# GpSimd writes the ones beside batch 2's and 3's value rows, batch 3's loads stand earlier, and pair 2's maxima stand behind the masks of pairs 0 and 1

## The chip, the cores and the metric

One Trainium2 chip, one core. The metric is the device time of one launch in microseconds (us); lower is better. The times of the kernel before are three runs; the profile is one more execution.

## What is computed

The inputs are q, k and v of shape (4, 8, 768, 64) (batch, heads, sequence, head size) and the weights of a gated layer. The reference, cut to what matters:

```python
k_sum = k.reshape(B, H, nb, 32, D).max(axis=3)      # 24 block maxima
v_sum = v.reshape(B, H, nb, 32, D).mean(axis=3)     # 24 block means
scores_l = scale * q @ k.T, kept only where |i - j| < 16
scores_s = scale * q @ k_sum.T + log(32)
a = softmax(concat([scores_l, scores_s]))
x = a @ concat([v, v_sum])                          # heads side by side: (3072, 512)
h = x @ w_in;  g = h * sigmoid(beta * h);  out = g @ w_out
```

d_model is 512 and d_ff is 2048. All matmuls run in bf16, the output is float32.

## The kernel before

The four batches run one after the other, and the work of batch b+1's attention is woven into batch b's two big matmuls. Heads are handled in pairs: pair g of a batch holds heads 2g and 2g+1, so there are four pairs. For each batch TensorE (PE) runs `h_group` (x times w_in, 16 groups, L509) and then `o_part` (times w_out, 24 parts, L530). On this main list a side list of small steps is laid: `at_time(t, f, ...)` puts step f at a planned time t, the list is sorted by t, and each step is emitted ahead of the first main step whose planned time is not below t. The planned times are only numbers that set an order: each engine then runs its own instructions in that order and waits for semaphores. `up` is the planned end of the h groups of the batch.

For batches 2 and 3 (while batch 1 or 2 is in the big matmuls) the steps of one pair are:

- `load_next` (on GpSimd, "POOL", which issues the DMAs that cast float32 to bf16): `load_v` brings value rows into `ve` (L118, the first and last rows apart in L126 and L124), `load_row` brings k and q rows in natural layout (L111, two DMAs each, 96 KB each). In front of pair 0 the columns `D:VW` of rows 96 to 127 of `ve` are set to one, so that the matmul that averages v also sums. There are two `ve` buffers, so batch 3's rows replace batch 1's, and four buffers each for k rows and q rows, so batch 3's pair g replaces batch 2's pair g.
- `copy_v` (on SyncE's queue, "SP"): two DMAs copy `ve` into `vo`, shifted by half a chunk (L328).
- `cross` (SP): two transposing DMAs bring k and q rows into `kw` and `qt` (L303, L305).
- `max_k` and `rows_k` (VectorE, "DVE"): the block maxima of the keys (L311, L313), then two copies that build the second set of key rows (L319, L320).
- `mean_v` (PE, L340) and `rows_v` (DVE, L347 and L353): block means of v, written into rows 96 to 127 of `ve` and `vo`.
- `scores` for two pairs (PE, L438, then exp on ScalarE, "ACT", L440), `mask` (DVE, L447), `av` (PE, L464), `norm` (DVE, L473 and L474), and `x_transpose` (SP, a transposing DMA into `xT`, L483). `xT` of all four pairs is what the next batch's h groups read; pair g is the g-th of the four products that are summed.

`scores` takes three accumulators and each `av` one, all from the same three "big" buffers, so the next `scores` needs `norm` of the `av` before it. SP also issues the stores of the output rows (L551), in its own order. The first two h groups of a batch are begun with pairs 0 to 2 only and finished with pair 3.

The block that plans batches 2 and 3 (`nxt` is the batch that is prepared; L685 to L703):

```python
elif nxt is not None:
    for g in pairs:
        at_time(0.1 + 0.2 * g, copy_v, nxt, g)
        at_time(0.2 + 0.2 * g, cross, nxt, g)
        m = 3.9 + 3.9 * g if g < 3 else up + 2.0
        at_time(m, max_k, nxt, g)
        at_time(m, rows_k, nxt, g)
    at_time(14.0, mean_v, nxt, pairs)
    for g in pairs:
        at_time(14.1 + 1.0 * g, rows_v, nxt, g)
    for g0, t, a in ((0, up + 0.8, up + 5.9), (2, up + 9.0, up + 14.5)):
        at_time(t, scores, nxt, g0)
        for g in (g0, g0 + 1):
            at_time(t, mask, nxt, g)
            at_time(a, av, (nxt, g), 0, nch)
        for g in (g0, g0 + 1):
            at_time(a, norm, (nxt, g), nch)
            at_time(a, x_transpose, (nxt, g), 0, nch, "big", dve)
```

Of the kernel before, what the change touches and what calls it, by code (L numbers as in the profile page):

```python
# [12 lines left out]
def kernel(  # L13
# [10 lines left out]
    nc = tc.nc  # L24
    ctx.enter_context(tc.manual_schedule(engines={getattr(mybir.EngineType, e) for e in ("SP", "Pool", "PE", "DVE", "Activation")}))
    P = 128
# [5 lines left out]
    B, H, S, D = q.shape  # L32
# [15 lines left out]
    VW = D + 1  # L48
# [7 lines left out]
    SUM = 96  # L56
# [18 lines left out]
    HC = H * nch  # L75
    PC = 2 * nch
    ve_bufs = [const.tile([P, HC + 1, VW], bf16, name=f"ve{i}") for i in range(2)]
# [30 lines left out]
    def load_row(nm, b, g):  # L108
        t = qk_pool.tile([P, nch, 2, D], bf16, name=nm + "_nat", tag=nm + "_row")
        for h in range(2):  # L110
            nc.gpsimd.dma_start(out=t[:, :, h], in_=(k_row if nm == "k" else q_row)[b, g, :, h])  # L111
        nat[(nm, b, g)] = t

    def load_v(b, g, n=1):
        lo, hi = PC * g + 1, min(PC * (g + n) + 1, HC)
        rows = v[b].rearrange("h s d -> (h s) d")
        src = rows[lo * P - W:hi * P - W].rearrange("(c p) d -> p c d", p=P)
        nc.gpsimd.dma_start(out=ve_bufs[b % 2][:, lo:hi, 0:D], in_=src)  # L118

    def load_v_edge(b, last):  # L120
        ve = ve_bufs[b % 2]
        rows = v[b].rearrange("h s d -> (h s) d")
        if last:
            nc.gpsimd.dma_start(out=ve[0:W, HC, 0:D], in_=rows[H * S - W:H * S])  # L124
        else:
            nc.gpsimd.dma_start(out=ve[W:P, 0, 0:D], in_=rows[0:P - W])  # L126
# [370 lines left out]
    def h_group(u, i, ks=range(k1)):  # L497

        b, t0, w = units[u]
        nn = 2 // w  # L500
        if 0 in ks:
            if (i * nn) % (k2 // w) == 0:
                h_bufs[(u, i * nn * w // k2)] = moe_pool.tile([P, k2 // w, w * MG], bf16, name="h_sb", tag="h_sb", bufs=4)
            h_open[(u, i)] = ps.tile([P, 2, 512], f32, name="h_ps", tag="big", bufs=3)
        big = h_open[(u, i)]
        for j in range(2):
            ni, tok = (i, t0 + j * MG) if w == 2 else (2 * i + j, t0)
            for ki in ks:
                nc.tensor.matmul(big[:, j, 0:MG], w_in_sb[:, ki, ni * P:(ni + 1) * P], xT[b][:, ki, tok:tok + MG],  # L509
                                 start=(ki == 0), stop=(ki == k1 - 1))  # L510
        if k1 - 1 not in ks:
            return
        for j in range(nn):
            ni = i * nn + j
            hb = h_bufs[(u, ni * w // k2)][:, ni % (k2 // w)]
            nc.scalar.activation(out=hb.rearrange("p (k m) -> p k m", m=MG), in_=big[:, j:j + w, 0:MG],  # L516
                                 func=ACTF.Silu, scale=beta_sb[:, ni:ni + 1])
# [119 lines left out]
    for b in range(B):  # L637
        us = [u for u, z in enumerate(units) if z[0] == b]
        up = sum(NG[u] for u in us) * GT
        total = up + nch * 4 * OT  # L640
        nxt = b + 1 if b + 1 < B else None
        pairs = tuple(range(npair))
        side = []

        def at_time(t, f, *a):
            side.append((t, lambda: f(*a)))

        if b == 0:
            for g in pairs:
                t = 3.9 if g < 2 else 6.5  # L650
                at_time(0.6 + 1.3 * g, mask_half, g)
                at_time(0.6 + 1.3 * g, rows_v, 0, g, HM, nch)
                if g % 2 == 0:
                    at_time(t, av_pair, g)
                at_time(t, norm, (0, g, 1), HM)
                at_time(t + 2.6, x_transpose, (0, g, 1), HM, HM, "t", dve)
            at_time(7.0, fill_band, 0, HM)
            at_time(7.0, band_edge, False)
            for n in range(k2):
                at_time(up - 7.5 + 0.4 * n, scale_w_out, n)  # L660
        if nxt == 1:
            for g in pairs:
                if g < 2:
                    p = up - 9.0 + 4.5 * g
                    at_time(p, prep_k, 1, g, "t")
                    at_time(p, prep_q, 1, g, "t", dve)
                    at_time(p + 0.8, copy_v, 1, g)
                else:
                    p = (up + 6.1, up + 7.8)[g - 2]
                    at_time(up + 0.5, cross, 1, g)  # L670
                    at_time((up + 4.0, up + 6.1)[g - 2], copy_v, 1, g, 0, nch, act)
                at_time(p, top_k, 1, g)
                at_time(p, rows_k, 1, g)
            at_time(up + 3.4, mean_v, 1, pairs, "big")
            for g0, t, r, a, xt in ((0, up + 0.3, up + 3.4, up + 7.7, 0.1), (2, up + 12.9, up + 12.9, up + 17.2, 2.6)):
                at_time(t, scores, 1, g0)
                for f in (rows_v, mask):
                    for g in (g0, g0 + 1):
                        at_time(r, f, 1, g)
                for g in (g0, g0 + 1):  # L680
                    at_time(a, av, (1, g), 0, nch)
                for g in (g0, g0 + 1):
                    at_time(a, norm, (1, g), nch)
                    at_time(a + xt, x_transpose, (1, g), 0, nch, "big", dve)
        elif nxt is not None:  # L685
            for g in pairs:

                at_time(0.1 + 0.2 * g, copy_v, nxt, g)
                at_time(0.2 + 0.2 * g, cross, nxt, g)
                m = 3.9 + 3.9 * g if g < 3 else up + 2.0  # L690
                at_time(m, max_k, nxt, g)
                at_time(m, rows_k, nxt, g)
            at_time(14.0, mean_v, nxt, pairs)
# [10 lines that stand above are left out]
        if nxt is not None:  # L704
            if nxt + 1 < B:
                def load_next(b, g):
                    if g == 0:
                        nc.vector.memset(ve_bufs[b % 2][SUM:P, 0:HC, D:VW], 1.0)
                        load_v_edge(b, False)
                    load_v(b, g)  # L710
                    if g == npair - 1:
                        load_v_edge(b, True)
                    load_row("k", b, g)
                    load_row("q", b, g)

                def open_gate():

                    nc.vector.memset(gate[:], 0.0)
                    nc.gpsimd.memset(gate[:], 0.0)

                if b == 0:
                    at_time(up + 6.0, open_gate)
                for g in pairs:
                    at_time(up + 6.0 + 0.01 * (g + 1) if b == 0 else 16.0 + 3.0 * g, load_next, nxt + 1, g)
        main = []
        for j, u in enumerate(us):
            for i in range(NG[u]):
                ks = range(k1 - 1, k1) if j == 0 and i < 2 else range(k1)
                main.append(((j * NG[u] + i) * GT, lambda u=u, i=i, ks=ks: h_group(u, i, ks)))
        for j, u in enumerate(us):  # L730
            n = units[u][2] * HM
            main += [(up + (4 * (j * n + ms) + p) * OT, lambda u=u, ms=ms, p=p: o_part(u, ms, p, 4)) for ms in range(n) for p in range(4)]
        if nxt is not None:
            main += [(total + i, lambda i=i: h_group(us[-1] + 1, i, range(k1 - 1))) for i in range(2)]
        side.sort(key=lambda z: z[0])
        for t, f in main:
            while side and side[0][0] <= t:
                side.pop(0)[1]()
            f()
        for _, f in side:  # L740
            f()
# [30 lines left out]
```

## Time and profile before

| | |
|---|---|
| median of three runs | 214.78 us (214.31 to 214.82) |
| the profiled execution's own time | 213.45 us |
| its span, first to last instruction | 211.8 us |
| PE busy | 202.3 us (96%) |
| DVE, ACT, POOL busy | 87.6, 116.7, 66.3 us |
| granted TensorE clock | 0.998 |

1.65 us of the profiled time lie outside the span. A share of busy time over 1 for DMA means that an engine had more than one packet under way. Busy PE is 96% on average, so what can still move the time is the few places where it waits.

### The profile page before, as it was taken

To read this page: it belongs to the slowest core of one execution; us is meant where nothing else is said; L and a number is where in the kernel's file an instruction comes from. 1 tells how busy PE (TensorE), PEld (TensorE's weight loads), DVE (VectorE), ACT (ScalarE), POOL (GpSimd) and SP (SyncE) were. 2 spreads that over 40 slices of the span, in tenths; PEclk is the share of its full clock that TensorE was granted. 3 is DMA by queue.
4 is the path that set the end of the run, shared out by engine and by line. 5 is a ranking of instruction groups with operands and counts; after the bars stand their busy time and mean duration, and the time that the engine had idled before them with its cause. 6 is when DMAs were issued, how large, how long until landed. Compare 5 with 4: busy or idle time off the path is not lost.

```text
span 211.8 us, 4839 instructions
## 1 busy us (share of the span) xinstructions
PE 202.3 (96%) x2005; PEld 113.3 (54%) x2024; DVE 87.6 (41%) x221; ACT 116.7 (55%) x159; POOL 66.3 (31%) x88
## 2 busy tenths in 40 slices
PE   7999999999999999999999699999999999999992
PEld 2656666654545556554545356555545565644452
DVE  3778891883796402229734002634634000002121
ACT  3799758889534376577161366678161576630000
POOL 7984344353397663004994400000000000000000
PEclk9999999999999999999999999999999999999999
DMA  6999999999999999993999999920344300001222
GB/s 179 184 151 193 204 205 206 185 178 167 162 192 142 227 199 172 143 141 61 170 145 206 170 218 152 202 41 0 100 126 109 117 0 3 0 2 65 83 91 61
DMA packets 93622, 28.34 MB, mean 134 GB/s; under 512 B 82256, under 2 KB 90656, under 8 KB 93600
## 3 DMA queue, kind: packets, MB, share of 16 engines
q0 software_dynamic: 63184, 13.24, 78.2%
q1 hardware_dynamic: 29968, 14.26, 34.3%
q10 hardware_dynamic: 448, 0.52, 0.8%
q8 instruction: 16, 0.26, 0.5%
q14 instruction: 6, 0.05, 0.1%
HBM read 27.27 MB, written 6.29 MB: 159 GB/s over the span
## 4 chain that ended last, share of the span: by engine, by line
PE 84%; DMA 6%; DVE 4%; ACT 2%; issue 2%
PE h_ps L509 40%; PE o_ps L530 30%; DMA xT<-x_nat 3%; PE av_ps L464 2%; DMA kw<-k_nat 2%; PE w_ps L560 2%; PE s_ps L438 2%; DVE x_nat L474 1%; DVE km L293 1%; PE px L488 1%; PE vm_ps L340 1%; ACT attn L440 1%; PE pq L279 1%; PE pk L279 1%; PE s_ps L383 1%
## 5 line engine op out<-in xcount | busy, mean ns | idle before, releaser
L509 PE MATMUL h_ps<-xT,w_in_sb 128*128 128x384 bf16 x512 | 85.9, 326 | 1.7 <-DMA xT<-x_nat 1.6
L530 PE MATMUL o_ps<-w_out_sb,h_sb 128*128 128x512 bf16 (+2 forms) x383 | 82.9, 370 | 2.0 <-issue 1.6
L516 ACT ACTIVATE h_sb<-h_ps,beta_sb 128x768 bf16<-128x768 f32 (+1 forms) x80 | 59.4, 773 | 25.1 <-PE h_ps L509 25.0
L509 PEld LDWEIGHTS <-w_in_sb 128*128 128x128 bf16 x512 | 49.4, 98 | 34.9 <-issue 2.1
L530 PEld LDWEIGHTS <-h_sb 128*128 128x128 bf16 x400 | 37.5, 98 | 41.6
L550 ACT COPY o_sb<-o_ps 128x512 f32<-128x512 f32 x18 | 10.7, 592 | 32.7 <-PE o_ps L530 21.1
L118 POOL DMA_DIRECT2D ve<-in_v_dram x12 | 14.3, 1195 | 24.3 <-PE o_ps L530 16.2
L440 ACT ACTIVATE attn<-s_ps 128x1024 bf16<-128x1024 f32 x18 | 17.1, 1024 | 7.0 <-PE s_ps L438 7.0
L111 POOL DMA_DIRECT2D k_nat<-in_k_dram x20 | 17.0, 858 | 10.8 <-DMA w_out_sb<-in_moe_w_out_dram 4.6
L550 DVE COPY o_sb<-o_ps 128x512 f32<-128x512 f32 x5 | 3.5, 692 | 39.5 <-PE o_ps L530 39.5
L111 POOL DMA_DIRECT2D q_nat<-in_q_dram x20 | 16.7, 845 | 7.3 <-DMA ve<-in_v_dram 3.7
L311 DVE TENSOR_TENSOR half<-kw 128x384 bf16<-128x384 bf16 x8 | 2.9, 357 | 37.3 <-DMA kw<-k_nat 37.3
L447 DVE TENSOR_TENSOR attn<-attn,band 128x1536 bf16<-128x1536 bf16 x12 | 11.1, 957 | 13.5 <-ACT attn L440 13.4
L474 DVE TENSOR_TENSOR x_nat<-av_ps,r 128x768 bf16<-128x768 f32 (+1 forms) x20 | 16.0, 798 | 0.7
L293 DVE TENSOR_REDUCE km<-kw 128x24 bf16<-128x768 bf16 x8 | 7.6, 948 | 1.8 <-DMA kw<-k_nat 0.9
L464 PEld LDWEIGHTS <-attn 128*64 128x64 bf16 x336 | 6.0, 111 | 3.0 <-issue 2.0
L473 DVE RECIPROCAL r<-av_ps 128x12 f32<-128x12 f32 (+1 forms) x20 | 4.2, 212 | 7.3 <-PE av_ps L464 6.9
L298 DVE COPY qt<-pq 128x768 bf16<-128x768 bf16 x5 | 4.8, 958 | 5.2 <-PE pq L279 5.1
L464 PE MATMUL av_ps<-vo,attn 128*64 128x65 bf16 x168 | 6.8, 196 | 0.0
L464 PE MATMUL av_ps<-ve,attn 128*64 128x65 bf16 x168 | 6.8, 196 | 0.0
L399 ACT ACTIVATE attn<-s_ps 128x768 bf16<-128x768 f32 x8 | 6.1, 808 | 0.7 <-PE s_ps L383 0.6
L560 PE MATMUL w_ps<-warm 128*128 128x512 bf16 x11 | 4.9, 611 | 1.3 <-DVE warm L156 1.3
(92 smaller groups left out, 139.5 us busy)
## 6 DMA issues: line engine op xcount, KB each, us to landing
out_dram<-o_sb SPq DMA_DIRECT2D x23, 256.0 KB, 3.9
w_out_sb<-in_moe_w_out_dram POOLq DMA_DIRECT2D x4, 512.0 KB, 17.3
k_nat<-in_k_dram POOLq DMA_DIRECT2D x20, 96.0 KB, 9.9
q_nat<-in_q_dram POOLq DMA_DIRECT2D x20, 96.0 KB, 10.8
w_in_sb<-in_moe_w_in_dram POOLq DMA_DIRECT2D x3, 512.0 KB, 13.8
ve<-in_v_dram POOLq DMA_DIRECT2D x6, 192.0 KB, 7.9
vo<-ve SPq DMA_DIRECT2D x10, 97.5 KB, 6.7
ve<-in_v_dram POOLq DMA_DIRECT2D x2, 384.0 KB, 12.7
```

The costliest lines, as they stand in the source:

```text
L111: nc.gpsimd.dma_start(out=t[:, :, h], in_=(k_row if nm == "k" else q_row)[b, g, :, h])
L118: nc.gpsimd.dma_start(out=ve_bufs[b % 2][:, lo:hi, 0:D], in_=src)
L293: nc.vector.tensor_reduce(out=km_of[g], in_=keys_of(b, g).rearrange("p (n f) -> p n f", f=block), op=ALU.max, axis=mybir.AxisListType.X)
L440: nc.scalar.activation(out=flat[:, j * n:(j + 1) * n].rearrange("p c h f -> p h c f"), in_=sv, func=ACTF.Exp, scale=scale)
L447: nc.vector.tensor_mul(out=a, in0=a, in1=band.rearrange("p r m h f -> p (r m h f)"))
L464: nc.tensor.matmul(ov[par * QT:(par + 1) * QT, h, m], a[:, par, m, h], t[:, PC * g + nch * h + m0 + m], start=True, stop=True)
L474: nc.vector.tensor_mul(out=x.rearrange("p m h d -> p h m d"), in0=ov[:, :, :, 0:D], in1=r[:, :, :, None].to_broadcast([P, 2, n, D]))
L509: nc.tensor.matmul(big[:, j, 0:MG], w_in_sb[:, ki, ni * P:(ni + 1) * P], xT[b][:, ki, tok:tok + MG], start=(ki == 0), stop=(ki == k1 - 1))
L516: nc.scalar.activation(out=hb.rearrange("p (k m) -> p k m", m=MG), in_=big[:, j:j + w, 0:MG], func=ACTF.Silu, scale=beta_sb[:, ni:ni + 1])
L530: nc.tensor.matmul(o_ps[:, c0:c1], h_bufs[(u, ni * w // k2)][:, ni % (k2 // w), ms * P:(ms + 1) * P], w_out_sb[:, ni, c0:c1], start=(ni == ...
L550: (nc.scalar.copy if u + 1 < len(units) else nc.vector.tensor_copy)(out=o_sb[:], in_=o_ps[:])
L560: nc.tensor.matmul(w_ps[:, 0], warm[:, 0:P], warm, start=True, stop=True)
```

## The change

Three edits. First, the two `max_k`/`rows_k` steps of pair 2 (for batches 2 and 3) go from planned time 11.7 to `up + 1.0`, and those of pair 3 from `up + 2.0` to `up + 1.0`, so both stand behind `scores` and `mask` of pairs 0 and 1, which are planned at `up + 0.8`. Second, the ones in `ve` are written by POOL and not by DVE (batches 2 and 3). Third, batch 3's four `load_next` steps are planned at 8.0, 11.5, 15.0 and 18.5 and not at 16, 19, 22 and 25.

```diff
-                m = 3.9 + 3.9 * g if g < 3 else up + 2.0
+                m = 3.9 + 3.9 * g if g < 2 else up + 1.0
                 at_time(m, max_k, nxt, g)
                 at_time(m, rows_k, nxt, g)
...
                     if g == 0:
-                        nc.vector.memset(ve_bufs[b % 2][SUM:P, 0:HC, D:VW], 1.0)
+                        nc.gpsimd.memset(ve_bufs[b % 2][SUM:P, 0:HC, D:VW], 1.0)
                         load_v_edge(b, False)
...
-                    at_time(up + 6.0 + 0.01 * (g + 1) if b == 0 else 16.0 + 3.0 * g, load_next, nxt + 1, g)
+                    at_time(up + 6.0 + 0.01 * (g + 1) if b == 0 else 8.0 + 3.5 * g, load_next, nxt + 1, g)
```

PE, ACT and SP keep their instructions and their order. On DVE, while batch 2 is prepared (kw_86, kw_87 are the key rows of pairs 1 and 2, vm_116 the means, ve_81 the value rows):

```order
@@ -128,8 +127,4 @@
 L319 COPY kw_86<-kw_86 128x6x96
 L320 COPY kw_86<-km_113 128x2x6x24
-L311 TENSOR_TENSOR half<-kw_87 128x384
-L313 TENSOR_REDUCE km_114<-half 128x24
-L319 COPY kw_87<-kw_87 128x6x96
-L320 COPY kw_87<-km_114 128x2x6x24
 L347 CAST vm_116<-vm_ps 128x130
 L353 COPY ve_81<-vm_116 32x780
```

Pair 2's four instructions leave their place ahead of the means of v. A little later on the same engine (kw_88 is pair 3's):

```order
@@ -143,4 +137,8 @@
 L353 COPY vo_83<-vm_116 32x780
 L447 TENSOR_TENSOR attn<-attn,band 128x1536 x2
+L311 TENSOR_TENSOR half<-kw_87 128x384
+L313 TENSOR_REDUCE km_114<-half 128x24
+L319 COPY kw_87<-kw_87 128x6x96
+L320 COPY kw_87<-km_114 128x2x6x24
 L311 TENSOR_TENSOR half<-kw_88 128x384
 L313 TENSOR_REDUCE km_115<-half 128x24
```

They come back behind the two masks, right ahead of pair 3's, which already stood there. Batch 3 moves in the same way. On POOL, at the start of batch 3's loads (ve_82 is the other value buffer; DMASW and DMAHW are transfers of POOL's and SP's queues, and the numbers behind the names are not times):

```order
-L126 DMA ve_82<-in_v_dram 112x64 [waits DMAHW5_49,DMASW7_49,PE_49]
-L118 DMA ve_82<-in_v_dram 128x12x64 [waits DMAHW6_49,DMASW0_49,DMAHW7_49,DVE_49,PE_49]
+L708 MEMSET ve_82 32x48 [waits DMAHW5_49,DMAHW7_49,DVE_49,PE_49]
+L126 DMA ve_82<-in_v_dram 112x64 [waits DMASW7_49]
+L118 DMA ve_82<-in_v_dram 128x12x64 [waits DMAHW6_49,DMASW0_49,Pool_49]
 L111 DMA k_nat<-in_k_dram 128x6x64 [waits DMAHW7_49,DMASW1_49]
```

The order of POOL's DMAs is as before; what moves is the write of the ones, from DVE's row to the head of POOL's, and with it the wait. Before, the first large load waited for DVE's write of the ones, which stood among the copies of L353. Now POOL waits for the last earlier users of `ve_82`, which are batch 1's.

## The prediction

> **What bounds the kernel now.** I read the page first, then the waits of PE alone, then the chain that ended last.
>
> ```profile
> PE 202.3 (96%) x2005; PEld 113.3 (54%) x2024; DVE 87.6 (41%) x221; ACT 116.7 (55%) x159; POOL 66.3 (31%) x88
> PE h_ps L509 <- DMA xT<-x_nat: 1.6, 1, 1.6
> 112.14 0.96 DVE x_nat L474
> ...
> 113.13 7.17 DMA xT<-x_nat
> ```
>
> PE is the bound, and past the start-up it waits for data in one place: batch 2's h groups wait 1.6 us for the last two transposes of x (pairs 2 and 3). The chain leaves PE there, goes over `norm` on DVE, and spends 7.17 us in a transposing DMA, to 120.30. The next rows are PE's timeline there, and the same place one batch later.
>
> ```profile
> 118.20 0.49 PE L509 MATMUL h_ps<-xT,w_in_sb 128*128 128x384 bf16 x2
> 120.34 14.30 PE L509 MATMUL h_ps<-xT,w_in_sb 128*128 128x384 bf16 x86 [1.65 <-DMA xT<-x_nat]
> ...
> 166.13 9.10 PE L509 MATMUL h_ps<-xT,w_in_sb 128*128 128x384 bf16 x55
> xT<-x_nat SPq DMA_TRANSPOSE x2, 2.7
> ```
>
> PE stops at 118.69 and resumes at 120.34. One batch later nothing waits: there the same two transposes land in 2.7 us (the last row, of the stretch 161 to 166). The difference is what else the DMA engines do. POOL's timeline (the first two rows of batch 3's loads) and DVE's write of the ones:
>
> ```profile
> 81.53 0.55 POOL L126 DMA_DIRECT2D ve<-in_v_dram  x1 [0.17 <-PE h_ps L509]
> 98.27 1.08 POOL L118 DMA_DIRECT2D ve<-in_v_dram  x1 [16.19 <-PE o_ps L530]
> 97.28 0.10 DVE L708 MEMSET ve<- 32x48 bf16 x1
> ```
>
> POOL sits idle for 16.19 us. The view names PE, but the wait ends 0.9 us after DVE has written the ones, and this instruction does wait for DVE. So batch 3's loads but for the first are issued from 98.27 on, and are under way when the transposes are issued at 113.13. That is the 1.65 us the change can win, 0.8% of the time, and no more: nowhere else past 20 us does PE wait for what it moves.
>
> **The change part by part: when are the loads through?** The third edit and the second belong together. With the ones on POOL, its memset can run at 81.5, since all it waits for is batch 1's. From then each row load waits for `cross` of the batch before (its buffer), so issue follows the crosses. What counts is when the DMA engines have finished. The DMA view counts packets per queue: q0 is POOL's, q1 SP's. The rows below are, in order: 81 to 90; 90 to 100, SP's queue; 98 to 102; then 98 to 113, 113 to 120 and 120 to 134, which together hold all of batch 3's loads; 104 to 106, where POOL's queue is alone; and 118.5 to 121.5, both queues, where loads run beside a transpose.
>
> ```profile
> q0 software_dynamic: 3685, 0.46, 82.3%
> q1 hardware_dynamic: 3389, 0.99, 73.4%
> q0 software_dynamic: 1104, 0.14, 54.9%
> q0 software_dynamic: 8527, 1.07, 126.8%
> q0 software_dynamic: 4674, 0.59, 131.0%
> q0 software_dynamic: 5455, 0.68, 80.8%
> q0 software_dynamic: 2394, 0.30, 240.7%
> q1 hardware_dynamic: 1264, 0.32, 80.5%
> q0 software_dynamic: 1260, 0.16, 80.3%
> ```
>
> Batch 3's loads are 8,527 + 4,674 + 5,455 = 18,656 packets. Alone the queue moves 2,394 in 2 us, 1,197 per us; beside a transpose both move one for one, about 420 per us. Now fill the hole. From 90 to 100 SP's 3,389 packets, one for one, take 3,389/421 = 8.0 us and let as many loads through; the other 2.0 us at 1,197 let about 2,330 through: 5,720. From 100 to 102 the queue would run full, 2,394, where it moved 1,104: 1,290 more. At 113 the loads are then 7,010 ahead: 18,656 - 8,527 - 7,010 = 3,120 left. At the pace of 113 to 120 (4,674/7 = 668 per us) that is 4.7 us, so the loads are through at 117.7.
>
> The bounds: at worst the hole only takes the pace of 81 to 90, 3,685/9 = 409 per us, so 4,090 in 10 us; 6,040 left at 668 per us take 9.0 us, to 122. At best SP's queue ahead of the transposes clears sooner too, and they land 2.7 us after issue, as in batch 3.
>
> The pair 2 transpose lands at 120.30 now. Its pair's x is 768 tokens by 128 columns in bf16, 197 KB; at the row's 0.32 MB in 1,264 packets that is about 770 packets, and at 421 per us 1.8 us, from about 118.5. With the loads through at 117.7 it runs alone and takes about half of that (estimate), so that it lands at about 119.3: **1.0 us of the 1.65 goes.** If the loads end at 122, nothing goes; at best 1.65. I take 1.0, as the one-for-one rows are of this very stretch.
>
> **What the first edit does on DVE.** Its rows around batch 2's attention, then batch 3's, then exp on ACT for both, then two copies of L319, and PE's next scores:
>
> ```profile
> 98.74 1.83 DVE L447 TENSOR_TENSOR attn<-attn,band 128x1536 bf16<-128x1536 bf16 x2
> 100.48 0.35 DVE L311 TENSOR_TENSOR half<-kw 128x384 bf16<-128x384 bf16 x1
> 102.13 0.23 DVE L473 RECIPROCAL r<-av_ps 128x12 f32<-128x12 f32 x1
> 103.53 0.96 DVE L474 TENSOR_TENSOR x_nat<-av_ps,r 128x768 bf16<-128x768 f32 x1
> 145.99 1.87 DVE L447 TENSOR_TENSOR attn<-attn,band 128x1536 bf16<-128x1536 bf16 x2 [6.39 <-ACT attn L440]
> 96.09 2.85 ACT L440 ACTIVATE attn<-s_ps 128x1024 bf16<-128x1024 f32 x3
> 144.02 2.85 ACT L440 ACTIVATE attn<-s_ps 128x1024 bf16<-128x1024 f32 x3
> 95.05 0.30 DVE L319 COPY kw<-kw 128x576 bf16<-128x576 bf16 x1
> 101.34 0.61 DVE L319 COPY kw<-kw 128x576 bf16<-128x576 bf16 x1
> 105.17 0.87 PE L438 MATMUL s_ps<-qt,kw 64*128 64x64 bf16 x48
> ```
>
> Before, the means of v and the masks queue behind pair 2's maxima. After, the masks start when exp allows: in batch 3 that is 145.99 - 144.02 = 1.97 us after its start, so 98.06 here and not 98.74. Behind them stand two sets of maxima and not one, 102.13 - 100.48 = 1.65 us each, then both norms (103.53 + 0.96 - 102.13 = 2.36). So the second norm ends at 104.49 - 0.68 + 1.65 = 105.46. PE's scores of pairs 2 and 3 need that accumulator for their last third, at 105.17 + 0.58 = 105.75: 0.29 us to spare. I book it at nothing. What hides it is that margin; a late copy of v (below) takes it away.
>
> One copy of L319 takes 0.61 us at 101.34 and 0.30 at 95.05; at the first POOL issues DMAs, at the second it is idle. The Trainium skill, page "VectorE: DVE Perf Modes", section "VectorE Performance Modes", says that VectorE's second port is shared with GpSimd and that 2-port instructions and GpSimd's block each other; the trace agrees by the doubled row. That speaks against the change: two sets of maxima now lie where POOL may still issue. The margin would be 0.31 us less, about nothing.
>
> **The memset on POOL** and the mean of v that waits for batch 2's rows. POOL's two nearest rows, then the last rows of v (issue, and us to landing in the next row), and PE's weights for the mean:
>
> ```profile
> 2.87 0.22 POOL masks.py:197 MEMSET identity<- 128x128 bf16 x1
> 55.40 0.10 POOL L719 MEMSET gate<- 1x16 f32 x1 [3.50 <-DVE gate L718]
> 75.01 0.53 POOL L124 DMA_DIRECT2D ve<-in_v_dram  x1 [0.36 <-DMA out_dram<-o_sb]
> ve<-in_v_dram POOLq DMA_DIRECT2D x1, 2.0 KB, 11.3
> 86.64 0.41 PEld L340 LDWEIGHTS <-A_avg 128*32 128x32 bf16 x28 [0.32 <-DMA ve<-in_v_dram]
> ```
>
> 32x48 elements lie between 1x16 and 128x128, so 0.10 to 0.22 us ahead of batch 2's loads. The last of them land at 75.01 + 11.3 = 86.3, the mean runs at 86.64: hidden, 0.1 us at most if not. On DVE the memset saves 0.10 us that nobody waits for.
>
> **The sum.** The profiled execution has 213.45 us (span 211.8 and 1.65 around it), 1.33 below the median of the runs. 213.45 - 1.0 = 212.45; on the median, 214.78 - 1.0 = **213.8 us**.
>
> **The rivals.**
>
> *The loads are still under way.* By the bound of 409 per us they end at 122; the transposes of 113 land where they do now, and the gain is 0 to 0.6 us: 214.2 to 214.8 on the median. For it: a busy share of 82.3% for q0 with no hole from 81 to 90, and crosses that the loads now meet. Against it: the 10 us from 90 hold only 8.0 us of SP's packets, and those at half pace. The skill's page "DMA: Bandwidth & Descriptors", section "Issuing engines are not separate DMA queues", has all queues run on the same 16 engines, so that issuing at once saves little; by it only the hole counts, not the 16 us by which issue moves, and the one-for-one rows agree.
>
> *Slower: SP's queue runs in order and starts late.* The v copies of batch 2, pair 3 (issue, then us to landing, and the slowest such copy in 82.5 to 85):
>
> ```profile
> 88.56 2.00 SPq L328 DMA_DIRECT2D vo<-ve  x2
> vo<-ve SPq DMA_DIRECT2D x1, 48.8 KB, 5.7
> vo<-ve SPq DMA_DIRECT2D x1, 48.8 KB, 8.7
> ```
>
> The second is issued about 89.6 and lands at 95.3. Among batch 3's loads it may take 8.7, to 98.3; the means of that pair then hold the masks to 99.0, and the second norm ends at 106.4: a stall of 0.65 us at the scores, and the x transposes of pairs 0 and 1 start with the norms, up to 106.4 - 104.49 = 1.9 us later, and push the stores and the transposes of pairs 2 and 3 behind them. If the loads are also still under way, the transpose of pair 2 lands up to 1.9 us later than 120.30; I take 1.2, as part of the delay is made up in SP's own gaps. PE then loses 1.2 us: 216.0 on the median. It decides from where that transpose lands past 120.9; a stall earlier costs nothing by itself while it is shorter than what the transposes still keep PE waiting.
>
> **How the numbers follow.** A measurement here can tell about 0.3%, 0.64 us, from no change, so faster means under 214.14 and slower over 215.42. The forecast (0.65 to 1.65 us won) has 0.52, the loads still under way 0.30, the late start 0.18. The forecast's own range is 213.1 to 214.1. The range given reaches 0.2 under it, since the runs spread 0.5, and up through the second case into the third, to its price: 212.9 to 216.0.
>
> **What would show it.** Right: POOL issues L118 at about 82.5 and is done by 105; q0 has packets through 90 to 100 and none after 118; the wait of L509 for xT falls from 1.65 to about 0.65 us; the second norm ends before 105.75. Wrong: q0 busy past 120 and that wait unchanged, or a new wait at L438 for L474, at L464 for L447, or at L340 for the rows of v.

## The result: no change that can be told, because the loads moved and did not finish early enough

| | before | after |
|---|---|---|
| median of 22 runs each | 214.59 us | 214.70 us |
| ratio of the runs, 95% interval | | 1.000 [0.9977, 1.0022] |
| the profiled execution's wait of L509 for xT | 1.65 us | 1.54 us |

Each ratio, here and below, is against runs of the kernel before taken beside it and leaves out the few runs that lie over 1.5% above the fastest of their kernel, so it is not the quotient of the medians.

The forecast of 213.8 us did not come about. The first rival did: the loads are still under way when the last two transposes of x run. The time lies in the range given, but for the rival's reason and not for the forecast's; the range spanned all three cases, no change among them.

The profile after. First the page's line of PE and two lines of its waits, then PE's timeline around the wait (start, length, engine, line, operation, count, and in brackets the idle time before with what ended it):

```profile
PE 202.8 (95%) x2005; PEld 113.6 (53%) x2024; DVE 87.8 (41%) x219; ACT 116.7 (55%) x159; POOL 66.8 (31%) x90
PE h_ps L509 <- DMA xT<-x_nat: 1.5, 1, 1.5
PE s_ps L438 <- DMA qt<-q_nat: 0.8, 1, 0.8
...
87.80 0.59 PE L340 MATMUL vm_ps<-ve,A_avg 128*32 128x130 bf16 x28
119.36 0.49 PE L509 MATMUL h_ps<-xT,w_in_sb 128*128 128x384 bf16 x2
121.39 14.37 PE L509 MATMUL h_ps<-xT,w_in_sb 128*128 128x384 bf16 x86 [1.54 <-DMA xT<-x_nat]
135.69 0.59 PE L340 MATMUL vm_ps<-ve,A_avg 128*32 128x130 bf16 x28
```

PE's busy share is 95% (96% before), and the wait is where it was, 0.1 us shorter. PE comes to it 1.16 us later than in the profile of before (119.36 against 118.20). That much was lost ahead of the stage the change acts on, 0.8 us of it in a wait at L438 that some of the executions below show and others don't, whether or not they have the change.

To compare executions without that spread, I take one stage: from the end of PE's mean of v for batch 2 to the end of the same for batch 3. After, it is 135.69 - 87.80 = 47.89 us. The two rows of before:

```profile
86.64 0.59 PE L340 MATMUL vm_ps<-ve,A_avg 128*32 128x130 bf16 x28
134.57 0.59 PE L340 MATMUL vm_ps<-ve,A_avg 128*32 128x130 bf16 x28
```

Before it is 47.93 us. The change leaves the stage as long as it was.

POOL's timeline shows that the loads did move. The last row is the last load of batch 3:

```profile
80.83 0.36 POOL L708 MEMSET ve<- 32x48 bf16 x1
81.92 0.56 POOL L126 DMA_DIRECT2D ve<-in_v_dram  x1 [0.74 <-DMA vo<-ve]
82.83 1.05 POOL L118 DMA_DIRECT2D ve<-in_v_dram  x1 [0.35 <-issue]
87.49 1.64 POOL L111 DMA_DIRECT2D k_nat<-in_k_dram  x2 [3.62 <-DMA ve<-in_v_dram]
...
111.90 0.82 POOL L111 DMA_DIRECT2D q_nat<-in_q_dram  x1 [0.39 <-DMA k_nat<-in_k_dram]
```

The first large load goes out at 82.83 and not at 98.27, 15.4 us earlier. The waits behind it name earlier loads of POOL's own queue that have yet to land (the listing of the change has them as waits for DMASW), so here issue goes no faster than the transfers, and the last load is issued at 111.90 where it was 119.96. The DMA view says what was moved. In order: 90 to 100 (POOL's queue), 98 to 102 (SP's), 100 to 113 (both), 113 to 120 and 120 to 134 (POOL's):

```profile
q0 software_dynamic: 5033, 0.63, 141.0%
q1 hardware_dynamic: 1343, 0.37, 79.6%
q0 software_dynamic: 7801, 0.98, 144.6%
q1 hardware_dynamic: 2507, 0.84, 69.9%
q0 software_dynamic: 3002, 0.38, 85.3%
q0 software_dynamic: 2423, 0.30, 33.5%
```

At 113, 3,002 + 2,423 = 5,425 packets are left, against 10,129 before. But the transposes are issued from 114.3 on, and the rest goes with them: the last of it, 590 packets, between 124 and 125. The transposes land 7.3 us after issue (the median of the two), in before 7.4.

### The profile page after: what moved, and what is told of

The parts are those of the page before. It is cut to its first block, busy times and chain, and to the rows that moved or that the text cites. A ratio compares the mean times of both kernels' runs of the same rounds, so it can differ in the third digit from the quotient of the medians.

```text
span 212.9 us, 4838 instructions
## 1 busy us (share of the span) xinstructions
PE 202.8 (95%) x2005; PEld 113.6 (53%) x2024; DVE 87.8 (41%) x219; ACT 116.7 (55%) x159; POOL 66.8 (31%) x90
## 4 chain that ended last, share of the span: by engine, by line
PE 84%; DMA 9%; issue 2%; DVE 2%; ACT 1%; SPq 0%; POOL 0%; POOLq 0%
PE h_ps L509 39%; PE o_ps L530 33%; DMA xT<-x_nat 4%; DMA qt<-q_nat 3%; DMA q_run<-in_q_dram 3%; PE av_ps L464 2%; PE s_ps L438 2%; PE vm_ps L340 1%; PE px L488 1%; DVE x_nat L474 1%; PE pq L279 1%; PE pk L279 1%; PE s_ps L383 1%; PE av_ps L411 1%; PE s_ps L378 1%
## 5 line engine op out<-in xcount | busy, mean ns | idle before, releaser
L509 PE MATMUL h_ps<-xT,w_in_sb 128*128 128x384 bf16 x512 | 85.9, 326 | 1.6 <-DMA xT<-x_nat 1.5
L509 PEld LDWEIGHTS <-w_in_sb 128*128 128x128 bf16 x512 | 49.2, 98 | 35.0 <-issue 2.1
L474 DVE TENSOR_TENSOR x_nat<-av_ps,r 128x768 bf16<-128x768 f32 (+1 forms) x20 | 16.0, 798 | 0.7
L353 DVE COPY ve<-vm 32x780 bf16<-32x780 bf16 x12 | 4.9, 408 | 4.7 <-DMA vo<-ve 4.4
L438 PEld LDWEIGHTS <-kw 64*128 64x128 bf16 x288 | 4.7, 95 | 3.4 <-issue 2.0
```

The costliest lines, as they stand in the source:

```text
L438: nc.tensor.matmul(sv[:, h, c], kw_of(b, g)[lo:lo + D, par, m, :], qt_bufs[g][lo:lo + D, m, par], start=True, stop=True)
L474: nc.vector.tensor_mul(out=x.rearrange("p m h d -> p h m d"), in0=ov[:, :, :, 0:D], in1=r[:, :, :, None].to_broadcast([P, 2, n, D]))
```

## The experiments

Theory A: the 1.5 us are the price of batch 3's loads that are under way beside the transposes of pairs 2 and 3, and the change moved them too little. Theory B: SP's own queue (stores, copies and crosses ahead of the transposes) holds the transposes, and the loads hardly matter. "Held" below means that some of batch 3's k and q rows are issued only when batch 2's last norms are done, behind a write that POOL waits for.

**Batch 3's loads left out.** The changed kernel; batch 3 uses rows of earlier batches again, so its results are not the reference's.

```diff
...
+                    if b == 3:
+                        return
                     load_v(b, g)
```

> The changed kernel without batch 3's loads: its v rows, k rows and q rows are not brought in, and batch 3 is computed from what its buffers hold (so 24 DMAs of POOL and 18,656 packets are left out). Theory A (the loads under way at 113 to 121 are what makes the x transposes of pairs 2 and 3 land late): the wait of L509 for xT, 1.5 us in the changed kernel, is gone (under 0.2), the transposes land in about 2.7 us, ratio to the kernel before about 0.993. Theory B (SP's own queue, the stores ahead of the transposes, makes them late): the wait stays over 1.0 us, ratio 0.998 to 1.002.

212.67 us, ratio 0.993 [0.990, 0.9961]. PE's timeline (L512 is L509 of the other kernels, three lines down), and the transposes in the DMA view of 113 to 120:

```profile
118.89 5.36 PE L512 MATMUL h_ps<-xT,w_in_sb 128*128 128x384 bf16 x32
...
xT<-x_nat SPq DMA_TRANSPOSE x2, 2.7
```

There is no idle time in front of the h groups, and the transposes land in 2.7 us instead of 7.3. SP still issues all that it did. Theory B falls; the loads are the cause.

**Rows of pairs 2 and 3 held (nothing left out).**

```diff
-                    load_row("k", b, g)
-                    load_row("q", b, g)
+                    if b == 2 or g < 2:
+                        load_row("k", b, g)
+                        load_row("q", b, g)
...
+                at_time(up + 6.0 if b == 0 else up + 14.6, open_gate if b == 0 else late_rows)
```

`late_rows` opens the gate and then loads the rows left out above.

> The changed kernel with batch 3's k and q rows of pairs 2 and 3 (3,072 packets each) held back behind a gate until the norms of batch 2's pairs 2 and 3; nothing is left out. Theory A: about 12,500 packets are through by 113, the transposes of x then run nearly alone, the wait of L509 falls from 1.5 to under 0.3 us, and the rows held back still arrive 20 us before the scores of pairs 2 and 3 need them: ratio 0.992 to 0.994. Theory B: wait over 1.0 us, ratio 0.998 to 1.002.

212.25 us, ratio 0.9898 [0.9867, 0.993]: the lowest median of this study, and more of a gain than Theory A's range. PE's timeline, then POOL's queue and the transposes in the DMA view of 113 to 120:

```profile
118.96 5.36 PE L509 MATMUL h_ps<-xT,w_in_sb 128*128 128x384 bf16 x32
...
q0 software_dynamic: 1348, 0.17, 38.0%
xT<-x_nat SPq DMA_TRANSPOSE x2, 3.5
```

The wait is gone with all loads done, only later. POOL's queue moves 1,348 packets in that stretch instead of 3,002, none of them before 117, and the transposes land in 3.5 us. The stage takes 45.96 us, to within 0.01 us what it takes without any loads of batch 3.

**Only pair 3's rows held.**

Against the hold just shown (`late_rows` then loads pair 3 alone):

```diff
-                    if b == 2 or g < 2:
+                    if b == 2 or g < 3:
```

> The changed kernel with the rows of pair 3 alone held back. Theory A: 15,600 packets aren't held and some 13,000 of them are through by 113, so about 2,500 (4 to 5 us) are under way beside the transposes; the wait of L509 lies between those of the full hold (0) and of the changed kernel (1.5), 0.4 to 1.2 us; ratio 0.993 to 0.997. Rival (any hold frees the queue): wait under 0.2 us.

213.20 us, ratio 0.9936 [0.9899, 0.9973]. PE's timeline, then POOL's queue and the transposes, again of 113 to 120:

```profile
120.06 4.19 PE L509 MATMUL h_ps<-xT,w_in_sb 128*128 128x384 bf16 x24 [0.40 <-DMA xT<-x_nat]
...
q0 software_dynamic: 1824, 0.23, 50.9%
xT<-x_nat SPq DMA_TRANSPOSE x2, 6.2
```

Half the held rows give a wait of 0.40 us, between 1.54 and none, at the low end of what Theory A expects.

**TensorE turns x.** Pairs 2 and 3 of batch 2 are transposed by PE and not by a DMA, so that no transfer stands between `norm` and the h groups. These two steps are also planned 2.6 later.

```diff
-        if b > 1 or (b == 1 and g < 2):
+        if b == 3 or (b > 0 and g < 2):
...
-                    at_time(a, x_transpose, (nxt, g), 0, nch, "big", dve)
+                    at_time(a + (2.6 if nxt == 2 and g0 == 2 else 0.0), x_transpose, (nxt, g), 0, nch, "big", dve)
```

> The changed kernel with batch 2's x of pairs 2 and 3 turned by TensorE (12 matmuls into a big accumulator, two copies on DVE) and not by transposing DMAs, as batch 1's are. Theory A: the wait of L509, 1.5 us, goes and 0.67 us of PE's time comes (12 matmuls, 71.55 minus 70.88 in the kernel before's chain): ratio 0.995 to 0.997. Rival (the loads hold up something else as well, such as the stores or batch 3's crosses): ratio 0.999 or more.

213.32 us, ratio 0.9942 [0.9921, 0.9964], a little better than expected. PE's timeline at the h groups:

```profile
120.35 3.90 PE L509 MATMUL h_ps<-xT,w_in_sb 128*128 128x384 bf16 x23
```

The wait is gone, with the loads where the change puts them. PE's own transposes add 0.67 us, so by the stage (46.62 us against 45.96) this is dearer than holding the rows. It says the same from the other side: what PE waits for is the landing of these two transfers.

**The first edit alone, and the second and third alone.**

```diff
-                m = 3.9 + 3.9 * g if g < 3 else up + 2.0
+                m = 3.9 + 3.9 * g if g < 2 else up + 1.0
```

The first run has this edit on the kernel before. The second has it the other way round on the kernel after.

> The kernel before with the first edit alone (pair 2's maxima behind the masks). Theory A: no change, ratio 0.998 to 1.002, the wait of L509 stays at 1.65 us; the second norm of batch 2 ends about 1.0 us later than before, against PE's scores. Rival (the first edit costs what the other two gain): slower, ratio 1.003 to 1.006, with a new wait of PE at the scores of pairs 2 and 3 or a longer wait for xT.

214.12 us, ratio 0.9993 [0.9966, 1.0019]. Waits of PE, then two rows of DVE, POOL's first large load and its last rows of batch 3, and POOL's queue in 100 to 113:

```profile
PE s_ps L438 <- DVE x_nat L474: 0.5, 1, 0.5
PE h_ps L509 <- DMA xT<-x_nat: 0.3, 1, 0.3
...
93.48 0.10 DVE L708 MEMSET ve<- 32x48 bf16 x1
103.43 0.90 DVE L320 COPY kw<-km 128x288 bf16<-128x288 bf16 x1
94.47 1.05 POOL L118 DMA_DIRECT2D ve<-in_v_dram  x1 [10.86 <-DVE ve L708]
110.67 1.77 POOL L111 DMA_DIRECT2D q_nat<-in_q_dram  x2
q0 software_dynamic: 12222, 1.54, 197.0%
```

I had not seen that the first edit moves the loads by itself: without pair 2's maxima in front, DVE writes the ones at 93.48 and not at 97.28, and POOL starts 3.8 us earlier. Theory A's forecast for the wait, 1.65 us, missed: it is 0.29. Here the stall that the prediction priced for the second norm appears, 0.46 us at L438: POOL issues while the maxima run, and the two sets take 4.07 us where they take 2.69 in the kernel after (L320 alone: 0.90 us). The two waits together are 0.75 us in this execution. The timed runs show no difference that can be told, though the stage of this one is 0.9 us shorter than before's, more than their interval allows; it is a single profile.

It shows something that the change hides. The loads start 11.6 us later here than in the kernel after, behind batch 2's crosses and not among them, and are issued without a pause. The last is out as early (the two of the row at 110.67, against 111.90), POOL's queue moves 12,222 packets in 100 to 113 against 7,801, and 3,419 are left at 113 against 5,425; they are through between 120 and 121. These two kernels differ by the second and third edit alone: in these executions the earlier start bought nothing and left more.

> The changed kernel with the first edit undone (loads early, ones on POOL, pair 2's maxima in their old place). Theory A: the loads end at about 125 as in the changed kernel, the wait of L509 stays at 1.3 to 1.7 us, ratio 0.998 to 1.003. Rival (the first edit costs what the loads gain): the wait of L509 falls below 0.9 us, ratio 0.994 to 0.997.

214.86 us, ratio 1.0006 [0.997, 1.0043], and the line of PE's waits:

```profile
PE h_ps L509 <- DMA xT<-x_nat: 1.7, 1, 1.7
```

The moved loads without the first edit change nothing that can be told. The first edit was not what kept the gain away.

**Rows held, in two other orders.** The same hold on the kernel before, and on the kernel after with the first edit taken back.

> The kernel before with the hold alone (batch 3's k and q rows of pairs 2 and 3 wait for batch 2's last norms); the loads still start at 98. Theory A (what counts is the packets of batch 3's loads still under way when the x transposes are issued at 113): the 12,500 packets that aren't held move at the kernel before's pace, 8,527 by 113, so some 4,000 are still under way, and the wait of L509 falls only to between 0.6 and 1.5 us; ratio 0.995 to 0.999. Rival (the hold alone is the gain, the early start gives nothing): wait under 0.2 us, ratio 0.990 to 0.994 as with the hold on the changed kernel.

> The changed kernel with the hold and with the first edit undone (pair 2's maxima back in their place). Theory A: the first edit does nothing for the transposes, so the wait of L509 is gone as with the hold, ratio 0.989 to 0.994. Rival (the maxima behind the masks let the masks start sooner and are part of the hold's gain): 0.5 us or more slower than the hold, with a wait of PE at the value product L464 for the masks L447.

The hold on the kernel before takes 212.73 us, ratio 0.9922 [0.990, 0.9945]. That is more of a gain than Theory A's 0.995 to 0.999 and lies in its rival's range: the early start adds nothing to the hold that can be told. On the kernel after without the first edit it takes 212.88 us, ratio 0.9927 [0.9899, 0.9955]. PE's timeline of the latter has no wait:

```profile
118.63 5.69 PE L509 MATMUL h_ps<-xT,w_in_sb 128*128 128x384 bf16 x34
```

The intervals of the three holds overlap: what helps is the hold, not the change. One thing did not fit. The profiled execution of the first of these took 214.77 us, the longest of its 12 runs, and showed the wait. So this kernel, before, after and the hold on the kernel after were profiled once more, unchanged.

> The kernel before with batch 3's k and q rows of pairs 2 and 3 held back, a second profiled execution. Theory A (the stall is the loads under way beside the last x transposes): the wait of L509 for xT is under 0.5 us here and the run takes about 212.7 us; the 1.56 us of the first profile belonged to a slow execution. Rival: the hold does not remove the wait in this order and the gain of its timed runs has another place; then the wait is again 1.2 to 2.0 us at about 212.7 us.

> The kernel before, a second profiled execution. Theory A: the wait of L509 for xT is there in every execution, 1.2 to 2.0 us, and the time is 214.0 to 215.5. Rival (the wait is chance, as the one for qt at L438 is): under 0.8 us.

> The changed kernel, a second profiled execution. Theory A: loads of batch 3 are still in POOL's queue past 120 and the wait of L509 for xT is 1.2 to 2.0 us; time 214.0 to 215.5. Rival (the first profile was a bad draw and the forecast's mechanism holds in others): the queue is empty by 120 and the wait is 0.4 to 0.9 us. The wait of L438 for qt near 63.5 is called chance: it may be there or not, 0 to 1 us.

> The changed kernel with batch 3's k and q rows of pairs 2 and 3 held back, a second profiled execution. Theory A: no wait of L509 for xT (under 0.2 us), time 212.0 to 213.0. Rival (its profile was a good draw): a wait of 0.5 us or more.

The h groups of the hold on the kernel before, first profile and second, and POOL's queue in 113 to 116 of each in the same order:

```profile
121.55 2.69 PE L509 MATMUL h_ps<-xT,w_in_sb 128*128 128x384 bf16 x14 [1.56 <-DMA xT<-x_nat]
119.88 4.38 PE L509 MATMUL h_ps<-xT,w_in_sb 128*128 128x384 bf16 x26 [0.45 <-DMA xT<-x_nat]
q0 software_dynamic: 1163, 0.15, 76.3%
q0 software_dynamic: 2331, 0.29, 154.2%
```

The second took 212.84 us, near the median of the timed runs, with a wait of 0.45. In the first, POOL's queue had moved half as many packets between 113 and 116 and then moved 2,353 between 116 and 120, against 1,381 in the second, while the transposes were under way. Why it was slower there stays open. Before and after, second execution (two lines of PE's waits each), and the hold on the kernel after (PE's timeline):

```profile
PE h_ps L509 <- DMA xT<-x_nat: 2.0, 1, 2.0
PE vm_ps L340 <- DMA ve<-in_v_dram: 1.5, 1, 1.5
```

```profile
PE h_ps L509 <- DMA xT<-x_nat: 1.8, 1, 1.8
PE vm_ps L340 <- DMA ve<-in_v_dram: 1.6, 1, 1.6
```

```profile
119.89 14.46 PE L509 MATMUL h_ps<-xT,w_in_sb 128*128 128x384 bf16 x88
```

Before and after (215.56 and 215.65 us) both have the wait in both executions, 1.65 and 2.04 against 1.54 and 1.83; the hold (213.17 us) has it in neither. All three took up to 0.2 us more than I had expected. A second wait, at L340 for batch 2's last value rows, appears in before and after alike (shorter in the hold), and in the first profile of neither.

The stage, from the rows of L340 as above (where a wait splits them, from the end of the last piece):

| kernel | stage, us | wait of L509, us |
|---|---|---|
| before, two executions | 47.93, 48.15 | 1.65, 2.04 |
| after, two executions | 47.89, 48.11 | 1.54, 1.83 |
| loads moved without the first edit | 47.98 | 1.70 |
| first edit alone | 47.03 | 0.29, and 0.46 at L438 |
| pair 3's rows held | 46.65 | 0.40 |
| TensorE turns x | 46.62 | none, but 0.67 of work |
| hold, kernel before, two executions | 47.93, 46.56 | 1.56, 0.45 |
| hold, without the first edit | 45.99 | none |
| hold, kernel after, two executions | 45.96, 45.95 | none |
| batch 3's loads left out | 45.95 | none |

## Why the prediction was wrong in its likeliest case, and right in its first rival

**What bounds the kernel: right.** One wait was to be won, and it is the loads that make it: without them, or with a third of their packets (6,144 of 18,656) held in the kernel after, it goes. The most that was to be had is more than the 1.65 us I gave, though: the stage is 47.93 - 45.96 = 1.97 us shorter when the wait is gone.

**The step that failed: "3,120 left ... at the pace of 113 to 120 (668 per us) that is 4.7 us, so the loads are through at 117.7".** Both its factors were off.

- What is left at 113. Measured 5,425, so 2,305 more. The hole from 90 to 100 took 5,033 packets where I had 5,720, which is 687 fewer; beside them SP's queue moved 2,332, where I had it move all its 3,389, one for one. The larger part is from 100 to 113: I took over the 8,527 packets of before and added 1,290, 9,817; it moved 7,801, which is 2,016 fewer. (About 400 had gone before 90.) SP's copies and crosses of batch 2 were slowed by the loads in the hole and ran on into that stretch: between 98 and 102 SP's queue carries 1,343 packets, before 73; over 100 to 113 it carries 2,507, before 1,839. The stretch itself had room, as the first edit alone shows with its 12,222 packets; what kept POOL's queue under that, beyond SP's share, stays open. The second execution divides it otherwise and ends the same. POOL's queue in 90 to 100, in 100 to 113, in 113 to 125, in 125 to 126:

```profile
q0 software_dynamic: 4235, 0.53, 123.9%
q0 software_dynamic: 9168, 1.15, 158.7%
q0 software_dynamic: 5033, 0.63, 92.4%
q0 software_dynamic: 371, 0.05, 72.2%
```

  There 5,404 are left at 113, within 0.5% of the first.
- The pace. Between 113 and 120 the rest went at 3,002/7 = 429 per us, not at 668. Both are means over unlike moments. Before, POOL's queue and SP's, from 117 to 118 and then from 119 to 120:

```profile
q0 software_dynamic: 1014, 0.13, 199.7%
q1 hardware_dynamic: 106, 0.03, 20.4%
q0 software_dynamic: 425, 0.05, 81.5%
q1 hardware_dynamic: 428, 0.10, 80.6%
```

  While the last transposes move, the second pace holds: in the kernel after the two queues move 413 and 414 packets between 119 and 120, 430 each in the next us and 416 each in the one behind it. At 429 the 3,120 packets would take 7.3 us, to 120.3 and not to 117.7. How much of the gain that would leave no run shows; the nearest is the first edit alone (3,419 left, waits of 0.75 us in all). I used the one-for-one price where it filled the hole and not where it emptied the queue.

So the loads end at 125 to 126, beyond even the worst end I gave (122), while the time is that of the rival with that bound. The Trainium skill, page "DMA: Bandwidth & Descriptors", section "Issuing engines are not separate DMA queues", says that transfers started by different engines run on the same 16 DMA engines and interleave, so that starting them side by side saves only the time of issuing. The trace agrees: issue moved by 15.4 us at its start, and the wait by 0.1 to 0.2 us.

**"Issue follows the crosses", "done by 105": wrong.** The waits in POOL's timeline name its own loads, up to 3.62 us, and the last issue is at 111.90.

**The first edit on DVE: right, to 0.6 us.** Rows of DVE after:

```profile
97.91 0.37 DVE L353 COPY ve<-vm 32x780 bf16<-32x780 bf16 x1 [3.69 <-DMA vo<-ve]
99.22 1.87 DVE L447 TENSOR_TENSOR attn<-attn,band 128x1536 bf16<-128x1536 bf16 x2 [0.67 <-ACT attn L440]
101.87 0.30 DVE L319 COPY kw<-kw 128x576 bf16<-128x576 bf16 x1
105.09 0.96 DVE L474 TENSOR_TENSOR x_nat<-av_ps,r 128x768 bf16<-128x768 f32 x1
```

The masks start at 99.22, which is the 98.06 I gave plus the 1.16 us by which PE is later in this execution. The second norm ends at 106.05; I had 105.46 + 1.16 = 106.62. The difference is that I priced each set of maxima with a copy of L319 that took 0.61 us, and both took 0.30 here, at 101.87 and 103.21, where POOL issues nothing. PE had no new wait at L438 for L474. The slower copies came in the first edit alone instead, and the wait with them. The rule I drew on there, that instructions of VectorE which use its second port and instructions of GpSimd block each other, stands in the Trainium skill on the page "Advanced Engine Details and Errata", section "VectorE Performance Modes", and not on the page I named. The trace agrees with it in both kernels: 0.72 us for L319 and 0.90 us for L320 where POOL issues, 0.30 and 0.23 us where it doesn't; but one copy of L319 beside POOL's issues, at 105.05 in the first edit alone, took 0.30 too.

**The slower rival: half of it came.** The copies of v did land late among the loads, and L353 waited 3.69 us for them. But exp on ACT, not L353, still released the masks (0.67 us), so nothing passed on.

**The memset: its price was too low, and its cover is thinner than I said.** It takes 0.31 to 0.36 us on POOL, over my 0.10 to 0.22. Ahead of batch 2's loads I called it hidden, 0.1 us at most if not. In the second executions L340 does wait for those rows, but 1.46 us before and 1.58 after; what the memset adds can't be told from so few.

## What to carry to other kernels

Issuing loads earlier could help here only by the packets that were through before the moment that counted. A start among other transfers slowed both and ended late; in one execution a start 11.6 us later, behind them, left fewer packets. Where a short transfer stands on the path, look at what is under way in the few microseconds around it: holding some of the loads back until it was issued was worth 0.7 to 1.0% here, moving them 15 us earlier nothing that can be told. And the pace for the packets that are left has to be that of the company they will have.

## What the runs showed of the hardware that was not expected

- One transposing DMA of a pair's x lands in 2.7 us without the loads and in 7.3 us among them, at the same place (medians of two).
- A stall of PE costs more than the idle time that the view lists. Against the stage without the wait (45.96), waits of 1.54, 1.65, 1.83 and 2.04 us cost 1.93, 1.97, 2.15 and 2.19 us, 0.15 to 0.4 us more. Some of it shows in PE's rows: the 88 matmuls take 14.46 us in one piece and 0.49 + 14.30 us in two.
- A copy of L320 takes 0.90 us where POOL issues DMAs beside it (first edit alone), and 0.23 us in the kernel after, where it doesn't.
- Executions of one kernel differ by waits of up to 1.6 us for transfers that were in time in others, at L340 and L438. A single profile doesn't show which waits are always there.
